# An attention and feed-forward kernel: another cycle of the engines' orders, and other places for the preparations

## The chip, the cores and the metric

The kernel runs on one core of a Trainium2 chip. The time is device microseconds of one execution; of several runs the median is given. The engines of the core are PE (matrix multiply), DVE, ACT and POOL (vector, scalar and general engines) and SP, which issues plain DMA transfers. POOL issues the transfers that add to what lies at their destination.

## The reference

Attention over pooled keys that are also the values, and a feed-forward layer with `h - tanh(h)` between its two products:

```python
kv_pool = kv.reshape(B, H // r, r, W // r, r, C).mean(axis=(2, 4))
k = v = kv_pool.reshape(B, -1, C) @ w_sr
s = scale * (q @ k.transpose(0, 2, 1))
a = np.exp(s - s.max(-1, keepdims=True))
a /= a.sum(-1, keepdims=True) + 1e-09
x = (a @ v).reshape(B * S, D)
h = x @ w_in
return (h - np.tanh(h)) @ w_out
```

B is 4, C is 128, there are 12288 queries and 768 pooled keys for each of the four batches, and the inner width of the feed-forward layer is 2048.

## The kernel before

The 49152 tokens are worked off in 96 groups of 512, 24 to a batch. For each group the kernel does an attention part and a feed-forward part, both written for small arguments: `exps` and `beyond` make the exponential less its straight part, and `square` and `cube` the cubic part of `h - tanh(h)`, while the straight parts are small products with matrices prepared for each batch (`Mh`, `Ah`).

In one group PE does 3 pairs of `scores` (L1073), 3 pairs of `values` (L1122), 8 pairs of `forth` (L1196), 8 pairs of `back` (L1234), two straight products of three (L1112, L1185) and `shares` (L1107), the sum of the attention weights. DVE does 3 `beyond` (L1080), 7 `cube` (L1203) and `apart` (L1133). ACT does 3 `exps`, 7 `square`, `copy`, and copies, among them `result` (L1245), the one that writes a group's output tile. POOL does the eighth piece of the feed-forward part (`moved_pool` L1210, and two `times` L1214, which write z and then rp), and three roundings: `rounded` (L1136), `lower_left` (L1165), `lower_q` (L1116).

For `shares` the three tiles of weights are first added up by transfers. SP copies the first to tile rs (L1093), POOL issues two transfers that add the second and the third to it (`added`, L1096), and from group 8 on one that adds its right half to its left (`folded`, L1099); each of them waits until the one before it has landed, since they write the same tile. `shares` reads the result.

The keys of the batches 1 to 3 are pooled by transfers too: SP loads the first of 16 pieces to tile kvp, and POOL issues 15 that add to it (`gather`, L604), one in each group, 15 groups in a row for each batch. Behind the last of them come the preparations of the batch: sums and products of the keys, the first-order step (`first`, `first_order`), slopes, `scaled` (L947, makes winr), `by_first` (L978, makes Wg) and `by_third` (L998, makes Wr).

The order of all instructions is set when the kernel is built. Each step is entered with a place (a number; 8 to a group), an engine, and a length; `Plan.run` lets the engines work by these lengths, and of the steps that could start it takes the one with the smallest place. The places of a group's steps stand in the table `AT`, those of preparations in `PLACES`; steps entered with `lane=True` keep the order of their places on their engine. An engine works off its steps strictly in the order that comes out of this: a step that waits holds up all that is behind it.

Of the kernel before, what the change touches and what calls it, by code (L numbers as in the profile page):

```python
# [46 lines left out]
class Plan:  # L47

    HOP = 0
# [3 lines left out]
    def __init__(self, tc, places):  # L53
        self.tc = tc
        self.ops, self.tiles, self.rings = [], {}, {}
        self.names = {}
        self.lanes = {}
        self.labels, self.places, self.moved, self.label_of = {}, places, {}, []
# [20 lines left out]
    def op(self, step, engine, us, emit, reads=(), writes=(), late=0.0, port=False, dma=0.0,  # L79
           name=None, lane=False):  # L80
        i = len(self.ops)
        label = self.label(emit, writes)
# [13 lines left out]
    def run(self, between):  # L96
        for t in self.tiles.values():
            i = t["by"][0][0] if t["by"] else None
# [31 lines left out]
        while any(ready.values()):  # L130
# [15 lines left out]
            if dma:  # L146
                free["dma"] = max(free.get("dma", 0.0), now + us) + dma
                late += free["dma"] - (now + us)
# [163 lines left out]
    "store_left left.3": 9.4781431, "copied rs.4": 9.4797277, "store": 9.4807533, "store 2": 9.6811954,  # L312
# [3 lines left out]
    "square W4": 20.156587, "straight acc.2": 20.1579222, "rows norms": 21.113721,  # L316
# [70 lines left out]
def attention_then_ffn(ctx: ExitStack, tc: tile.TileContext, q, kv_first, kv_by_key, kv_by_place,  # L387
# [650 lines left out]
    def attention(g, s0, s1):  # L1038
# [108 lines left out]
        if g >= FOLDED:  # L1147
            plan.op(s0 + AT["folded"], "POOL", 0.87 if g < SET else 0.65, folded, (rs,), (rs,), late=2.0, dma=0.3,
                    lane=True)
# [407 lines left out]
```

## Time and profile before

| what | value |
|---|---|
| median of 3 runs | 1343.48 us (1339.9 to 1345.6) |
| the profiled execution | 1343.29 us, span 1341.6 us |
| PE busy | 1265.1 us (94%) |
| DVE busy | 1209.6 us (90%) |
| ACT busy | 1204.6 us (90%) |
| POOL busy | 1225.6 us (91%) |
| adding transfers (queue q0) | 78.53 MB, 36.6% of the DMA engines' span |
| mean granted clock of PE | 0.997 |

The span is that of the instructions in the trace; the time of the execution holds a little more around it. The busy shares are means over stages of different kinds, so the rows further down cut the span into stages at the starts of `result`. On POOL the recorded spans of neighbours overlap by some tenths of a us, so there the distance from start to start is the length of a step.

### The profile page before, as it was taken

The numbers are of one execution on the slowest core, as the hardware profiler recorded it, in microseconds if no ns is written. First come the engines' busy times: TensorE is split into PE (matmuls) and PEld (weight loads), VectorE is DVE, ScalarE is ACT, GpSimd is POOL, SyncE is SP. The second block draws the span as 40 slices with busy tenths as digits, with TensorE's granted clock in tenths as the row PEclk, the third lists the DMA queues.
The fourth block names the chain that finished last, engine by engine and source line by source line (L and its number), as shares of the span: only waits on it lengthen the run. The fifth ranks groups of instructions, "written<-read, shape, count | busy, mean of one in ns | idle before, by whom it ended". The sixth has DMA issues, their size and how long they took to land.

```text
span 1341.6 us, 17444 instructions
## 1 busy us (share of the span) xinstructions
PE 1265.1 (94%) x5466; PEld 873.0 (65%) x5466; DVE 1209.6 (90%) x1171; ACT 1204.6 (90%) x1413; POOL 1225.6 (91%) x1069
## 2 busy tenths in 40 slices
PE   8999989998989889999989988999999999999997
PEld 6767666766756557666666666766666666666664
DVE  4999998888888888999989988899999999999996
ACT  3899998898889988999989988899999999999995
POOL 3799899999998988999999898899999999999996
PEclk9999999999999999999999999999999999999999
DMA  9286666456666664554666676354544545555541
GB/s 346 61 161 136 145 129 146 99 120 138 140 126 145 122 140 113 122 126 107 145 123 142 129 144 137 81 133 116 124 107 114 126 100 122 122 114 119 122 95 36
DMA packets 95621, 170.01 MB, mean 127 GB/s; under 512 B 11329, under 2 KB 24769, under 8 KB 95521
## 3 DMA queue, kind: packets, MB, share of 16 engines
q0 software_dynamic: 46224, 78.53, 36.6%
q1 hardware_dynamic: 49296, 90.29, 19.1%
q8 instruction: 45, 0.74, 0.2%
q14 instruction: 56, 0.45, 0.1%
HBM read 57.93 MB, written 25.39 MB: 62 GB/s over the span
## 4 chain that ended last, share of the span: by engine, by line
POOL 51%; PE 16%; DMA 15%; issue 11%; DVE 4%; ACT 2%; SPq 0%; POOLq 0%; ACTq 0%; DVEq 0%
POOL rp L1214 13%; DMA rs<-r 12%; POOL rs L1096 9%; POOL z L1214 8%; POOL z L1210 5%; PE big L1196 5%; POOL dl L1165 4%; PE acc L1234 4%; POOL rs L1099 4%; POOL ql L1116 3%; DVE r L1203 2%; POOL dr L1136 2%; PE big L1073 2%; PE x L1122 2%; POOL kvp L604 1%
## 5 line engine op out<-in xcount | busy, mean ns | idle before, releaser
L1203 DVE SCALAR_TENSOR_TENSOR r<-big,u 128x1024 fp32r<-128x1024 f32 x672 | 779.3, 1218 | 35.2 <-ACT u L1200 33.9
L1200 ACT ACTIVATE u<-big 128x1024 f32<-128x1024 f32 x672 | 660.0, 1031 | 45.7 <-PE big L1196 36.0
L1196 PE MATMUL big<-dr,winr 128*128 128x512 f32 x1536 | 531.1, 427 | 2.1 <-DVE r L1080 1.2
L1234 PE MATMUL acc<-r,Wr 128*128 128x512 f32 x1344 | 413.0, 398 | 0.6 <-DVE r L1203 0.6
L1080 DVE SCALAR_TENSOR_TENSOR r<-E,big 128x1024 f16<-128x1024 f32 x288 | 349.3, 1217 | 55.3 <-ACT E L1077 49.3
L1196 PEld LDWEIGHTS big<-dr,winr 128*128 128x128 f32 x1536 | 272.5, 189 | 103.2 <-DVE r L1203 26.0
L1077 ACT ACTIVATE E<-big 128x1024 f32<-128x1024 f32 x288 | 295.6, 1027 | 19.8 <-PE big L1073 13.0
L1234 PEld LDWEIGHTS acc<-r,Wr 128*128 128x128 f32 x1344 | 251.5, 189 | 59.1 <-DVE r L1203 1.5
L1214 POOL TENSOR_TENSOR rp<-z,v 128x1024 fp32r<-128x1024 f32 x96 | 289.5, 3016 | 0.2
L1214 POOL TENSOR_TENSOR z<-z,v 128x1024 f32<-128x1024 f32 x96 | 265.9, 2769 | 0.3
L1096 POOL DMA_DIRECT2D rs<-r x188 | 208.9, 1111 | 31.1 <-DMA rs<-r 13.5
L1073 PE MATMUL big<-qr,kTr 128*128 128x512 f32 x576 | 212.0, 450 | 0.4 <-ACT kTr L720 0.4
L1122 PE MATMUL x<-r,vvr 128*128 128x512 f16 x576 | 174.3, 385 | 0.0
L1116 POOL TENSOR_TENSOR ql<-q,qr 128x512 fp32r<-128x512 f32 x96 | 160.5, 1672 | 0.5 <-ACT qr L1057 0.5
L1165 POOL TENSOR_TENSOR dl<-df,dr 128x512 fp32r<-128x512 f32 x96 | 160.8, 1675 | 0.0
L1210 POOL TENSOR_SCALAR z<-v 128x1024 f32<-128x1024 f32 x96 | 124.5, 1297 | 12.6 <-ACT v L1207 11.9
L1073 PEld LDWEIGHTS big<-qr,kTr 128*128 128x128 f32 x576 | 102.6, 189 | 48.7 <-DVE r L1080 14.5
L1099 POOL DMA_DIRECT2D rs<-rs x88 | 87.9, 998 | 25.4 <-DMA rs<-r 24.4
L1234 PE MATMUL acc<-rp,Wr 128*128 128x512 f32 x192 | 67.2, 431 | 39.7 <-POOL rp L1214 39.3
L1207 ACT COPY v<-big 128x1024 f32<-128x1024 f32 x96 | 97.8, 1019 | 1.8 <-PE big L1196 1.6
L1245 ACT ACTIVATE o<-acc,At 128x512 f32<-128x512 f32 x96 | 65.8, 685 | 29.1 <-PE acc L1234 28.9
L1136 POOL TENSOR_SCALAR dr<-df 128x512 fp32r<-128x512 f32 x96 | 82.4, 858 | 2.7 <-DVE df L1133 2.7
(178 smaller groups left out, 1020.5 us busy)
## 6 DMA issues: line engine op xcount, KB each, us to landing
rs<-r POOLq DMA_DIRECT2D x188, 256.0 KB, 4.1
q<-in_q_dram SPq DMA_DIRECT2D x96, 256.0 KB
out_dram<-o SPq DMA_DIRECT2D x96, 256.0 KB
rs<-r SPq DMA_DIRECT2D x94, 256.0 KB
kvp<-in_kv_by_place_dram POOLq DMA_DIRECT2D x45, 384.0 KB, 5.5
rs<-rs POOLq DMA_DIRECT2D x88, 128.0 KB, 2.7
winr<-in_kv_first_dram SPq DMA_DIRECT2D x8, 384.0 KB
kc<-inverse SPq DMA_DIRECT2D x12, 256.0 KB
```

Of the source, the lines that this page charges most:

```text
L1073: PE.matmul(out=half(plan[s], h), lhsT=plan[kTr][:, n * P : (n + 1) * P], rhs=plan[qr], start=True, stop=True)
L1077: A.activation(out=plan[e], in_=plan[s], func=AF.Exp)
L1080: V.scalar_tensor_tensor(out=plan[r], in0=plan[e], scalar=-1.0, in1=plan[s], op0=ALU.add, op1=ALU.subtract)
L1096: PL.dma_start(out=plan[rs], in_=plan[r2s[k]], accum_op=ALU.add)
L1116: PL.tensor_tensor(out=plan[ql], in0=plan[qs], in1=plan[qr].bitcast(F32), op=ALU.subtract)
L1122: PE.matmul(out=plan[num], lhsT=plan[vvr][:, n], rhs=half(plan[f"r2.{g}.{k}"], h), start=(start and h == 0), stop=(stop and h == 1))
L1165: PL.tensor_tensor(out=plan[dl], in0=plan[df], in1=plan[dr].bitcast(F32), op=ALU.subtract)
L1196: PE.matmul(out=half(plan[hp], h), lhsT=plan[winr][:, f * P : (f + 1) * P], rhs=plan[dr], start=True, stop=True)
L1200: A.activation(out=plan[u], in_=plan[hp], func=AF.Square)
L1203: V.scalar_tensor_tensor(out=plan[r], in0=plan[hp], scalar=1.0, in1=plan[u], op0=ALU.add, op1=ALU.mult)
L1214: PL.tensor_tensor(out=plan[to], in0=plan[x], in1=plan[y], op=ALU.mult)
L1234: PE.matmul(out=plan[acc], lhsT=plan[Wr][:, 2 * n + h], rhs=half(plan[r], h), start=(start and h == 0), stop=(stop and h == 1))
```

## The change

The planner's rules get a queue of their own for transfers that add (`way`): such transfers follow one another there, each beginning no sooner than `AHEAD` behind its issue. The lengths and the times at which results are handed on are set to other values. The table `AT` of a group's places is replaced, and so is a part of `PLACES` (all entries of the preparations of the batches 1 to 3). No step is added or taken away, and no shape is changed.

```diff
-    HOP = 0
+    HOP, AHEAD = 0, 0.85
@@ class Plan, op
+        if way:
+            self.ways.add(i)
@@ class Plan, run
             if dma:
-                free["dma"] = max(free.get("dma", 0.0), now + us) + dma
-                late += free["dma"] - (now + us)
+                way, ahead = ("way", self.AHEAD) if i in self.ways else ("dma", 0.0)
+                free[way] = max(free.get(way, 0.0), now + us + ahead) + dma
+                late += free[way] - (now + us)
@@ PLACES
-    "scaled winr.1 2": 234.4723885, "by_third Wr.1 4": 243.982368, "by_first wg.1.2": 253.4967438,
+    "scaled winr.1 2": 230.002, "by_third Wr.1 2": 230.0025, "by_third Wr.1 4": 230.003,
@@ keys, gather
-            plan.op(at + (0.01 if w else -4), *(("POOL", 0.87 if b < 2 else 0.65) if w else ("SP", 0.5)), gather, (), (kvp,),
-                    late=3.0, dma=1.0, lane=w > 0)
+            if w:
+                plan.op(at + 0.01, "POOL", 0.607, gather, (), (kvp,), late=0.3, dma=3.5, lane=True, way=True)
+            else:
+                plan.op(at - 4, "SP", 0.5, gather, (), (kvp,), late=3.0, dma=1.0)
@@ AT
-        back=[10.761, 7.019, 7.331, 7.954, 6.395, 8.578, 9.358, 5.772], scores=[-20.616, -21.551, -19.32],
+        back=[10.776, 7.328, 7.019, 7.947, 6.399, 8.721, 9.34, 6.09], scores=[-20.605, -21.533, -19.303],
...
-        more=[6.696, 8.691], copied=-18.562, added=[-15.731, -13.315], folded=-9.726, shares=-7.11, left=-6.713,
+        more=[6.68, 8.666], copied=-18.551, added=[-15.755, -12.945], folded=-9.746, shares=-7.434, left=-6.705,
...
-        lower_q=-12.065, lower_left=3.108, gather=-5.737)
+        lower_q=-12.123, lower_left=2.23, gather=-4.52)
@@ attention
-                plan.op(s0 + AT["added"][k - 1], "POOL", 0.87 if g < SET else 0.65, partial(added, k), (r2s[k],), to,
-                        late=2.4, dma=0.6, lane=True)
+                plan.op(s0 + AT["added"][k - 1], "POOL", 0.638, partial(added, k), (r2s[k],), to, late=0.3, dma=1.8,
+                        lane=True, way=True)
...
-            plan.op(s0 + AT["folded"], "POOL", 0.87 if g < SET else 0.65, folded, (rs,), (rs,), late=2.0, dma=0.3,
-                    lane=True)
+            plan.op(s0 + AT["folded"], "POOL", 0.645, folded, (rs,), (rs,), late=0.3, dma=0.9, lane=True, way=True)
```

On POOL, a group with a gather (group 45), from behind the second `times` of the group before to its own, before:

```order
L604 DMA kvp<-in_kv_by_place_dram 128x768
L1096 DMA rs<-r_6938 128x1024
L1165 TENSOR_TENSOR dl<-df,dr 128x512
L1116 TENSOR_TENSOR ql<-q,qr 128x512
L1210 TENSOR_SCALAR z<-v 128x1024
L1136 TENSOR_SCALAR dr<-df 128x512
L1099 DMA rs<-rs 128x512
L1214 TENSOR_TENSOR z<-z,v 128x1024
L1096 DMA rs<-r_7040 128x1024
L1214 TENSOR_TENSOR rp<-z,v 128x1024
```

The same place in the changed kernel, whose line numbers are 4 to 6 higher:

```order
L1170 TENSOR_TENSOR dl<-df,dr 128x512
L1102 DMA rs<-r_6936 128x1024
L608 DMA kvp<-in_kv_by_place_dram 128x768
L1122 TENSOR_TENSOR ql<-q,qr 128x512
L1215 TENSOR_SCALAR z<-v 128x1024
L1142 TENSOR_SCALAR dr<-df 128x512
L1105 DMA rs<-rs 128x512
L1219 TENSOR_TENSOR z<-z,v 128x1024
L1102 DMA rs<-r_7035 128x1024
L1219 TENSOR_TENSOR rp<-z,v 128x1024
```

The step dl (`lower_left`) now stands ahead of the second `added`, and the gather behind it. A plain group reads the same without the gather's row.

On POOL, a group with a preparation (group 36, batch 2), its first six rows before:

```order
L998 TENSOR_TENSOR Wr<-wout_69,hb 128x512
L1096 DMA rs<-r_5671 128x1024
L1165 TENSOR_TENSOR dl<-df,dr 128x512
L1116 TENSOR_TENSOR ql<-q,qr 128x512
L1210 TENSOR_SCALAR z<-v 128x1024
L1136 TENSOR_SCALAR dr<-df 128x512
```

and now:

```order
L1170 TENSOR_TENSOR dl<-df,dr 128x512
L1102 DMA rs<-r_5676 128x1024
L1122 TENSOR_TENSOR ql<-q,qr 128x512
L953 TENSOR_TENSOR winr<-win_67,kc 128x512
L1215 TENSOR_SCALAR z<-v 128x1024
L1142 TENSOR_SCALAR dr<-df 128x512
```

The preparation stood ahead of the second `added` and of `lower_left`; now it stands behind `lower_q`, and it is another one of the batch.

On PE, any plain group from the straight product of the feed-forward part to `shares`, before:

```order
L1185 MATMUL acc<-dl,Ah 128x512
L1196 MATMUL big<-dr,winr 128x512 x2
L1234 MATMUL acc<-r,Wr 128x512 x2
L1196 MATMUL big<-dr,winr 128x512 x2
L1234 MATMUL acc<-r,Wr 128x512 x2
L1196 MATMUL big<-dr,winr 128x512 x2
L1234 MATMUL acc<-r,Wr 128x512 x4
L1196 MATMUL big<-dr,winr 128x512 x2
L1234 MATMUL acc<-r,Wr 128x512 x2
L1196 MATMUL big<-dr,winr 128x512 x2
L1234 MATMUL acc<-r,Wr 128x512 x2
L1107 MATMUL x<-rs,share 128x512
```

and now:

```order
L1190 MATMUL acc<-dl,Ah 128x512
L1201 MATMUL big<-dr,winr 128x512 x4
L1240 MATMUL acc<-r,Wr 128x512 x4
L1201 MATMUL big<-dr,winr 128x512 x2
L1240 MATMUL acc<-r,Wr 128x512 x4
L1201 MATMUL big<-dr,winr 128x512 x2
L1240 MATMUL acc<-r,Wr 128x512 x2
L1201 MATMUL big<-dr,winr 128x512 x2
L1113 MATMUL x<-rs,share 128x512
```

A second pair of `forth` goes ahead of the first `back`, and `shares` stands ahead of the `back` pair that it followed.

## Rows read from the trace of the kernel before

**Rows 1.** Windows by stage, instructions of L1245 alone: stretch, length, ACT busy (groups), clock, DMA.
```profile
96.90:133.60 36.70, 2.04 (x3) 1.00 0.65 141
146.30:227.50 81.20, 4.13 (x6) 1.00 0.67 136
227.50:315.80 88.30, 4.12 (x6) 0.98 0.52 119
315.80:498.80 183.00, 8.96 (x13) 1.00 0.65 134
498.80:650.00 151.20, 7.53 (x11) 1.00 0.52 121
650.00:827.90 177.90, 8.94 (x13) 1.00 0.66 135
827.90:1018.60 190.70, 9.60 (x14) 1.00 0.49 115
...
1108.40:1291.70 183.30, 10.22 (x15) 1.00 0.50 116
```
**Rows 2.** Windows, last stage: PE, PEld, DVE, ACT, POOL busy, clock, DMA.
```profile
1108.40:1291.70 183.30, 183.30 (x767) 124.06 (x766) 181.93 (x166) 180.99 (x211) 174.11 (x136) 1.00 0.50 116
```
**Rows 3.** Timeline of POOL, a gather group: start, us, what, [idle before it].
```profile
427.60 1.49 POOL L604 DMA_DIRECT2D kvp<-in_kv_by_place_dram  x1
429.31 0.85 POOL L1096 DMA_DIRECT2D rs<-r  x1 [0.21 <-issue]
429.87 1.61 POOL L1165 TENSOR_TENSOR dl<-df,dr 128x512 fp32r<-128x512 f32 x1
431.11 1.61 POOL L1116 TENSOR_TENSOR ql<-q,qr 128x512 fp32r<-128x512 f32 x1
432.37 1.36 POOL L1210 TENSOR_SCALAR z<-v 128x1024 f32<-128x1024 f32 x1
433.39 0.92 POOL L1136 TENSOR_SCALAR dr<-df 128x512 fp32r<-128x512 f32 x1
435.28 0.89 POOL L1099 DMA_DIRECT2D rs<-rs  x1 [0.96 <-DMA rs<-r]
435.92 2.67 POOL L1214 TENSOR_TENSOR z<-z,v 128x1024 f32<-128x1024 f32 x1
438.27 1.17 POOL L1096 DMA_DIRECT2D rs<-r  x1
438.88 2.98 POOL L1214 TENSOR_TENSOR rp<-z,v 128x1024 fp32r<-128x1024 f32 x1
441.23 1.46 POOL L604 DMA_DIRECT2D kvp<-in_kv_by_place_dram  x1
```
**Rows 4.** The chain that ended last, the same group: start, us, what.
```profile
429.31 5.68 DMA rs<-r
```
**Rows 5.** L1096 alone, 1150 to 1250 us (plain groups): landings.
```profile
DMA to landing us min/median/max: 3.3/3.6/4.8
```
**Rows 6.** Timeline of POOL, a plain group.
```profile
1164.56 1.21 POOL L1096 DMA_DIRECT2D rs<-r  x1
...
1168.73 0.88 POOL L1096 DMA_DIRECT2D rs<-r  x1 [0.51 <-DMA rs<-r]
...
1173.79 0.88 POOL L1099 DMA_DIRECT2D rs<-rs  x1
```
**Rows 7.** DMA issues, 360 to 500 us: count, size, median us to landing.
```profile
kvp<-in_kv_by_place_dram POOLq DMA_DIRECT2D x10, 384.0 KB, 5.5
rs<-rs POOLq DMA_DIRECT2D x10, 128.0 KB, 2.7
```
**Rows 8.** Groups by line: busy us, mean ns, idle before.
```profile
L947 POOL TENSOR_TENSOR winr<-win,kc 128x512 fp32r<-128x512 f32 x12 | 23.4, 1953 | 0.0
L998 POOL TENSOR_TENSOR Wr<-wout,hb 128x512 fp32r<-128x512 f32 x16 | 22.9, 1438 | 0.8 <-DVE wout L527 0.7
```
**Rows 9.** Timeline of PE, a plain group around the weights' sum.
```profile
1177.24 0.63 PE L1234 MATMUL acc<-r,Wr 128*128 128x512 f32 x2
1177.71 0.39 PE L1107 MATMUL x<-rs,share 128*128 128x512 f16 x1
```

More of the change, by code (lines that the diff above doesn't have):

```diff
@@ L57, in __init__ @@
         self.lanes = {}
+        self.ways = set()
         self.labels, self.places, self.moved, self.label_of = {}, places, {}, []
@@ L79, in op @@
     def op(self, step, engine, us, emit, reads=(), writes=(), late=0.0, port=False, dma=0.0,
-           name=None, lane=False):
+           name=None, lane=False, way=False):
         i = len(self.ops)
+        if way:
+            self.ways.add(i)
         label = self.label(emit, writes)
@@ L278 @@
     "load_words words.o.0": -154.3354073, "load planes.2 2": -149.679321, "load planes.0 2": -145.9573847,
[33 rows of a table removed]
-    "store_left left.3": 9.4781431, "copied rs.4": 9.4797277, "store": 9.4807533, "store 2": 9.6811954,
[3 rows of a table removed]
-    "square W4": 20.156587, "straight acc.2": 20.1579222, "rows norms": 21.113721,
[66 rows of a table removed]
[34 rows of a table added]
+    "straight acc.2": 20.1579222, "rows norms": 21.113721, "square p4.0": 21.4626768,
[69 rows of a table added]
 }
@@ L411, in attention_then_ffn @@
     PAIR, THREE = (0.465, 0.469), (0.7, 0.704)
-    PE_LATE, ACT_LATE, DVE_LATE = (0.196, 0.15), (0.14, 0.1), (0.2, 0.14)
+    PE_LATE, ACT_LATE, DVE_LATE, POOL_LATE = (0.196, 0.186), (0.14, 0.135), (0.2, 0.14), (0.0, 0.38)
     BUFS = {"kc": 2, "kvp": 1, "kTr": 2, "vvr": 2, "Mn": 1, "Mh": 2, "A": 2, "Ah": 2, "Wg": 3, "Wr": 2,
@@ L1028, in attention_then_ffn @@
     AT = dict(
-        forth=[4.008, 1.046, 1.669, 5.46, 0.266, 6.083, 6.707, -0.357],
-        first=[4.466, 1.603, 2.213, 5.871, 0.678, 6.495, 7.119, 0.064],
-        then=[5.134, 2.321, 3.075, 6.548, 1.566, 7.302, 8.057, 0.811],
-        back=[10.761, 7.019, 7.331, 7.954, 6.395, 8.578, 9.358, 5.772], scores=[-20.616, -21.551, -19.32],
-        exps=[-20.144, -21.139, -18.908], beyond=[-19.413, -20.17, -18.232], values=[-3.68, -4.927, -4.304],
-        more=[6.696, 8.691], copied=-18.562, added=[-15.731, -13.315], folded=-9.726, shares=-7.11, left=-6.713,
-        straight=-6.019, apart=-2.656, rounded=-2.118, rounded_q=-24.272, slope=4.992, result=11.47,
-        lower_q=-12.065, lower_left=3.108, gather=-5.737)
+        forth=[4.014, 1.031, 1.693, 5.471, 0.257, 5.78, 6.709, -0.362],
+        first=[4.484, 1.619, 2.225, 5.903, 0.689, 6.509, 7.141, 0.081],
+        then=[5.17, 2.351, 3.101, 6.598, 1.6, 7.349, 8.099, 0.85],
+        back=[10.776, 7.328, 7.019, 7.947, 6.399, 8.721, 9.34, 6.09], scores=[-20.605, -21.533, -19.303],
+        exps=[-20.122, -21.101, -18.871], beyond=[-19.396, -20.148, -18.176], values=[-3.676, -4.914, -4.295],
+        more=[6.68, 8.666], copied=-18.551, added=[-15.755, -12.945], folded=-9.746, shares=-7.434, left=-6.705,
+        straight=-5.998, apart=-2.643, rounded=-2.135, rounded_q=-24.253, slope=5.006, result=11.505,
+        lower_q=-12.123, lower_left=2.23, gather=-4.52)
     def attention(g, s0, s1):
@@ L1153, in attention @@
         plan.op(s1 + AT["left"] + 1, "SP", 0.5, store_left, (t,), (f"left.{g}",), late=2.0, dma=0.02)
-        plan.op(s0 + AT["lower_q"], "POOL", 1.29, lower_q, (qs, qr), (ql,), lane=True)
+        plan.op(s0 + AT["lower_q"], "POOL", 1.25, lower_q, (qs, qr), (ql,), late=POOL_LATE[g >= SET], lane=True)
         terms = [(AT["values"][k], PAIR[g >= SET], partial(values, k), (vvr, r2s[k])) for k in range(AN)]
@@ L1159, in attention @@
             plan.op(s1 + at, "PE", us, partial(emit, start=(n == 0), stop=(n == AN)), of, (num,),
-                    late=PE_LATE[g >= SET], lane=True)
+                    late=PE_LATE[g >= SET] if g < SET or n == AN else 0.0, lane=True)
         plan.op(s1 + AT["apart"], "DVE", 0.6 if g < SET else 0.63, apart, (num, t), (df,), late=DVE_LATE[g >= SET], lane=True)
-        plan.op(s1 + AT["rounded"], "POOL", 0.59, rounded, (df,), (dr,), lane=True)
+        plan.op(s1 + AT["rounded"], "POOL", 0.59, rounded, (df,), (dr,), late=POOL_LATE[g >= SET], lane=True)
         def lower_left():
             PL.tensor_tensor(out=plan[dl], in0=plan[df], in1=plan[dr].bitcast(F32), op=ALU.subtract)
-        plan.op(s1 + AT["lower_left"], "POOL", 1.29, lower_left, (df, dr), (dl,), lane=True)
+        plan.op(s1 + AT["lower_left"], "POOL", 1.25, lower_left, (df, dr), (dl,), late=POOL_LATE[g >= SET], lane=True)
     EARLY = (2.5, 4.4, 4, 6, 8, 18, 24, 8)
@@ L1222, in feed_forward @@
                 plan.op(first, "ACT", 0.905, copy, (hp,), (v,), late=ACT_LATE[g >= SET], lane=True)
-                plan.op(then, "POOL", 1.1, moved_pool, (v,), (z,), lane=True)
+                plan.op(then, "POOL", 1.1 if g < SET else 1.03, moved_pool, (v,), (z,), lane=True)
                 for to, at in zip((z, r), AT["more"]):
-                    plan.op(s0 + at, "POOL", 2.41, partial(times, to, z, v), (z, v), (to,), lane=True)
+                    plan.op(s0 + at, "POOL", 2.37, partial(times, to, z, v), (z, v), (to,),
+                            late=0.5 if to == r and g >= SET else 0.0, lane=True)
             else:
@@ L1241, in feed_forward @@
             plan.op(s0 + at, "PE", us, partial(emit, start=(n == 0), stop=(n == UN)), of, (acc,),
-                    late=PE_LATE[g >= SET], lane=True)
+                    late=PE_LATE[g >= SET] if g < SET or n == UN else 0.0, lane=True)
         def result():
```

203 rows, old and new, of the table PLACES are left out of this document.

## Prediction

> **What bounds the kernel now.** I read first how fast the groups of 512 tokens come out, stage by stage, and then asked in the slow stages which wait ends last. The windows that count the output copies (L1245, one per group) show it [rows 1]. In the last stage 15 groups take 183.3 us, 12.22 each. There PE is busy 183.3 of 183.3 us and DVE 181.9 [rows 2]: both are full, so 12.22 is the floor of a plain group and no order of POOL's work can beat it. Two stages hold nearly only plain groups that also carry one adding load of the keys (`gather`, L604): 6 groups in 81.2 us (13.5 each) and 13 in 177.9 us (13.7 each). Early in the program three groups have such loads too, but no `folded` (it starts with group 8); they take 36.7 us, 12.23 each. So the adding load costs 1.4 us where there is a fold and nothing where there is none: the loss is no bandwidth, it is a loop through the fold.
>
> POOL's order shows that loop [rows 3]. From one L1099 (`folded`) to the next: L1099 to `times` 0.64 us, `times` 2.35, first `added` 0.61, second `times` 2.35 (to the L604 at 441.23), L604 to the second `added` (L1096) 1.71 (427.60 to 429.31), and from that L1096 to the next L1099 5.97. Sum 13.63, the period. In the 5.97 POOL works 4.7 and then waits 0.96 for DMA rs<-r. The chain that ended last goes the same way: 5.68 us of DMA from the second `added` [rows 4]. Where no L604 stands ahead, the same transfer lands after a median of 3.6 us [rows 5], and POOL only waits for the first `added` (0.51 us) [rows 6]. So the load, which lands 5.5 us after its issue [rows 7], holds the `added` behind it for about 2 us, `folded` waits for that, and since POOL works in order everything behind `folded` waits too.
>
> **The change, part by part.** *The gather goes behind the second `added`.* In POOL's order `lower_left` comes up ahead of the second `added`, and the gather falls to just behind it. The loop is then 0.64 + 2.35 + 0.61 + 2.35 + 1.24 (`lower_left`, 429.87 to 431.11) + 3.6 (landing) + 0.3 (5.97 less 5.68, what stands between landing and L1099) = 11.1 us, below 12.22. What is next is POOL's own sum: 0.64 + 2.35 + 0.61 + 2.35 + 1.24 + second `added` 0.56 + gather 1.71 + `lower_q` 1.26 + `moved_pool` 1.02 + `rounded` about 0.6 (0.92 recorded, its record overlaps the next as the others do) = 12.3. The gather's price is the open one: 0.56, as an `added` between two vector steps costs, or 1.71, as the pair of transfers L604, L1096 shows. Two transfers still stand side by side, so I take 1.71. A gather group then takes 12.35 us.
>
> *Plain gather groups.* First stage: 81.2 - 6 x 12.35 = 7.1 us saved. The stage of 13 groups from 650.0: 177.9 - 160.6 = 17.3; I take 16, since the last product of the preparation's slopes moves into it by the new order.
>
> *Gather groups with preparations* (13 groups from 315.8, 183.0 us). POOL also has 4 `by_third`, 1 `by_first`, 3 `scaled` and two small steps there. By record L998 takes 1.44 us and L947 1.95 [rows 8]; less the overlap of 0.64 that the rows of group 3 show (recorded 2.98 and 2.35 apart), 0.8 to 1.3. Together 10 us. In the old order the loop had room for little of that, and with POOL full at 12.3 they now add in whole: 13 x 12.35 + 10 = 170.5; 12.5 saved.
>
> *The three stages without gathers for most groups* (6 groups from 227.5, 11 from 498.8, 14 from 827.9). Each begins with one or two gather groups, which save 1.3 each: 2.6, 3 and 3. The rest of their loss is the chain of the key sums, first-order steps and products on PE, DVE and POOL. Its steps stay the same in number; they are shuffled, with `scaled` and `by_third` now behind `lower_q` and not between the second `times` and the second `added`, so that `lower_left`, for which DVE's `apart` and PE's straight product wait, is not held up by them. I count nothing for it; between -4 and +4 us for each of the three stages is the bound.
>
> *Plain groups.* PE gets a second `forth` ahead of the `back` pairs, and `shares` one `back` pair earlier, 0.47 us (1177.24 to 1177.71) [rows 9]. DVE's and ACT's orders are the same in a plain group. Since DVE and PE are full there, I count no gain and no loss. `shares` needs the fold's landing: L1099 at 1173.79 [rows 6] plus 2.7 [rows 7] is 1176.5, and `shares` starts at 1177.71, so 1.2 us of cover; 0.7 remain.
>
> *Planner's numbers* (`AHEAD`, `way`, the `late` values) issue nothing; they act through the order alone.
>
> **Sum.** 7.1 + 16 + 12.5 + 2.6 + 3 + 3 = 44.2 us. The profiled execution took 1343.3 us (span 1341.6 and 1.7 around it), which is the median of the three runs, 1343.5. 1343.3 - 44.2 = 1299.
>
> **A page against the row.** The second `added` lands 5.68 us after its issue with a gather ahead, 3.6 without, and the gather itself in 5.5 [rows 4, 5, 7]. The Trainium skill ("DMA: Bandwidth & Descriptors", section on the anatomy of one DMA on the SWDGE path) fits a transfer of this path as 2.0 us plus bytes over 436 GB/s: an estimate from it is 2.9 us for 384 KB, so that a gather ahead would hold an `added` for 0.9 us at most. By that rule the old loop would be 0.64 + 2.35 + 0.61 + 2.35 + 1.71 + 3.5 = 11.2 us, it would bind nothing, and the new place would give nothing. This trace does not agree: adding transfers land later than the fit says, and the wait of 0.96 us is there.
>
> **The rivals.**
> (a) *`folded` behind the gather, `shares` late.* From 2.7 us for 128 KB and 3.6 for 256 KB an adding transfer moves 0.9 us per 128 KB after 1.8 of fixed time; the gather, 5.5, moves 3.7. With the second `added` issued at 0, it moves until 3.6, the gather until 7.3, and the fold, issued at about 0.56 + 1.71 + 1.26 + 1.02 + 0.6 = 5.15, lands at 7.3 + 0.9 = 8.2 where 7.85 would be undisturbed: 0.35 late, inside the cover of 0.7. For it: the margin is thin, and landings vary (3.3 to 4.8 in plain groups [rows 5]). If `shares` comes 0.6 us late in each of some 34 gather groups, PE waits 20 us: 1320.
> (b) *The order does not matter to the load.* If the gather holds up whatever is around it, `folded` still waits, at 13.5 a group; only the shuffle of preparations counts: 1343, and 1331 to 1355 at its bounds. Against it: the groups without folds run at 12.23 with the same loads.
> (c) *Slower: the fold's loop in plain groups.* Moving `lower_left` ahead takes 1.24 us from the time between the second `added` and `folded` in every group. The loop is 7.5 us plus the landing. With 3.6 it is 11.1; with a landing of 5.0 it reaches 12.5 and binds in the plain groups too. With x us a group everywhere, 52 plain groups lose x - 12.22 and 34 gather groups win 13.6 - x: the change loses from x = 12.77, a landing of 5.3 us. At 5.5 it gives x = 13.0 and 52 x 0.78 - 34 x 0.6 = +20: 1363. Against it: the largest landing in the plain stage is 4.8.
>
> **How the numbers follow.** Forecast 0.65; (a) 0.20; (b) 0.08; (c) 0.05; 0.02 for anything else. The likeliest case gives 1299; with the stages of preparation at their bounds 1287 to 1311. If all loss of the gather stages goes (7.9 + 24.1 + 19.0 us against 12.22) and the others give 12 in all, the time is 1280, the low end; (a) sets the high end, 1320. A run of this kernel tells about 0.5% from no change. Forecast and (a) are faster by more than that, (b) is the same, (c) slower: 0.87, 0.08, 0.05.
>
> **What would show it.** In the gather stages: 12.3 to 12.4 us a group; L1105, the new line of `folded`, no longer waits for DMA rs<-r; the `added` behind `lower_left` lands in about 3.6 us; POOL is busy nearly without gaps. (a) shows as PE waiting at `shares` for DMA rs<-rs, (b) as 13.5 a group, (c) as POOL waiting at `folded` in the last stage, with more than 12.22 a group there. The forecast is wrong if the last stage's period moves at all, since 0.1 us there is 5 to 9 us over the program, or if the preparations cost more in their new places than they did.

## The result, and the profile after

The changed kernel takes 1321.03 us (median of 4 runs, 1318.29 to 1322.75), the kernel before on the same chip 1343.78 (4 runs): a ratio of 0.9833 [0.9804, 0.9862], 1.7% faster. The forecast was 1299, its range 1280 to 1320: the gain has the forecast's sign and half its size, and the time lies just above the range, at the 1320 that rival (a) gave. The profiled execution took 1322.75 us, the slowest of the four (span 1321.0).

The windows of the changed kernel on `result`, now L1251, between the starts that answer to those of [rows 1] (stretch, length, ACT busy with the number of groups, clock, DMA):

```profile
145.90:226.30 80.40, 4.09 (x6) 0.98 0.67 138
226.30:311.60 85.30, 4.11 (x6) 1.00 0.54 122
311.60:488.30 176.70, 8.90 (x13) 0.99 0.66 139
488.30:640.10 151.80, 7.53 (x11) 1.00 0.52 120
640.10:806.60 166.50, 8.88 (x13) 1.00 0.69 144
806.60:999.30 192.70, 9.60 (x14) 0.99 0.49 113
1087.40:1271.30 183.90, 10.24 (x15) 1.00 0.50 116
```

The gain stands in three stages: the 13 gather groups (177.9 to 166.5 us), the 13 with preparations (183.0 to 176.7), and the second row (88.3 to 85.3). The six gather groups of the first row gain 0.8 only, chiefly since one of them (group 9) grew from 13.73 to 16.11 us, and the two long stages of preparations gain nothing.

POOL's timeline of one gather group, which answers to [rows 3] (start, us, what, idle time before it):

```profile
717.66 0.88 POOL L1102 DMA_DIRECT2D rs<-r  x1 [0.18 <-issue]
718.25 1.22 POOL L608 DMA_DIRECT2D kvp<-in_kv_by_place_dram  x1
718.81 1.97 POOL L1122 TENSOR_TENSOR ql<-q,qr 128x512 fp32r<-128x512 f32 x1
720.32 1.47 POOL L1215 TENSOR_SCALAR z<-v 128x1024 f32<-128x1024 f32 x1
721.34 1.04 POOL L1142 TENSOR_SCALAR dr<-df 128x512 fp32r<-128x512 f32 x1
721.90 1.34 POOL L1105 DMA_DIRECT2D rs<-rs  x1
722.54 3.15 POOL L1219 TENSOR_TENSOR z<-z,v 128x1024 f32<-128x1024 f32 x1
726.17 0.88 POOL L1102 DMA_DIRECT2D rs<-r  x1 [0.47 <-DMA rs<-r]
726.78 2.71 POOL L1219 TENSOR_TENSOR rp<-z,v 128x1024 fp32r<-128x1024 f32 x1
```

`folded` (L1105) waits for nothing here, and only once, for 0.6 us, in the stage's 13 groups (9.0 us in 10 groups before): the loop no longer binds. The waits of that stage (engine, line, what was waited for; us in total, times, the longest) show what came in its place:

```profile
PE x L1113 <- DMA rs<-rs: 6.4, 11, 1.1
PEld L1113 <- DMA rs<-rs: 5.7, 6, 1.5
...
POOL rs L1102 <- DMA rs<-r: 1.7, 4, 0.5
...
POOL rs L1105 <- DMA rs<-r: 0.6, 1, 0.6
```

PE now stands at `shares` (L1113) until the fold has landed, 6.4 us in 11 of the 13 groups. The row of PEld is the weight load of the same step: the same waits, seen from another row, and not to be added. PE's timeline, in the group above:

```profile
724.84 0.62 PE L1201 MATMUL big<-dr,winr 128*128 128x512 f32 x2
726.58 0.39 PE L1113 MATMUL x<-rs,share 128*128 128x512 f16 x1 [1.12 <-DMA rs<-rs]
726.62 0.82 PE L1240 MATMUL acc<-r,Wr 128*128 128x512 f32 x2
```

The landings in that stage, of the fold and of the gather (times from issue to landing):

```profile
L1105 POOL DMA_DIRECT2D rs<-rs x13: 876/1166/1417, 644.7 to 798.4; - x13
DMA to landing us min/median/max: 2.9/3.9/4.6
...
L608 POOL DMA_DIRECT2D kvp<-in_kv_by_place_dram x13: 1216/1529/1871, 640.4 to 794.1; - x13
DMA to landing us min/median/max: 6.4/6.9/7.4
```

The fold, 2.7 us from issue to landing in [rows 7], takes 3.9, and the gather 6.9 instead of 5.5. In the old order both transfers ahead of the fold had landed when it was issued: at 435.28 in [rows 3], against 433.1 (427.60 and 5.5) and 434.99 (429.31 and 5.68); now the gather is issued 0.59 us behind the `added`, and the fold 3.65 us behind the gather, which is still under way. In the last stage, which has no gathers, the busy times of PE, PEld, DVE, ACT and POOL are those of [rows 2]:

```profile
1087.40:1271.30 183.90, 183.46 (x768) 123.54 (x767) 181.98 (x166) 181.23 (x211) 174.63 (x138) 1.00 0.50 116
```

### The profile page after: what moved, and what is told of

Same layout as the page of the kernel before. It is cut to its first block, busy times and chain, and to the rows that moved or that the text cites. A ratio compares the mean times of both kernels' runs of the same rounds, so it can differ in the third digit from the quotient of the medians.

```text
span 1321.0 us, 17453 instructions
## 1 busy us (share of the span) xinstructions
PE 1263.0 (96%) x5466; PEld 877.6 (66%) x5466; DVE 1212.0 (92%) x1171; ACT 1202.6 (91%) x1413; POOL 1228.0 (93%) x1069
## 4 chain that ended last, share of the span: by engine, by line
POOL 47%; PE 29%; issue 9%; DMA 8%; ACT 4%; DVE 3%; POOLq 0%; ACTq 0%; DVEq 0%
POOL rp L1219 11%; POOL rs L1102 9%; PE big L1201 8%; POOL z L1219 8%; PE acc L1240 8%; POOL z L1215 5%; DMA rs<-r 4%; POOL ql L1122 4%; PE big L1079 4%; DMA rs<-rs 3%; PE x L1128 3%; POOL dr L1142 3%; POOL rs L1105 2%; POOL kvp L608 2%; PE x L1118 2%
## 5 line engine op out<-in xcount | busy, mean ns | idle before, releaser
L1201 PE MATMUL big<-dr,winr 128*128 128x512 f32 x1536 | 498.9, 416 | 1.5 <-DVE r L1208 0.5
L1219 POOL TENSOR_TENSOR rp<-z,v 128x1024 fp32r<-128x1024 f32 x96 | 284.2, 2961 | 0.2
L1219 POOL TENSOR_TENSOR z<-z,v 128x1024 f32<-128x1024 f32 x96 | 279.6, 2912 | 0.3
L1102 POOL DMA_DIRECT2D rs<-r x188 | 237.5, 1263 | 17.1 <-DMA rs<-r 13.9
L1079 PE MATMUL big<-qr,kTr 128*128 128x512 f32 x576 | 210.8, 447 | 0.4 <-ACT kTr L726 0.4
L1122 POOL TENSOR_TENSOR ql<-q,qr 128x512 fp32r<-128x512 f32 x96 | 201.9, 2103 | 0.5 <-ACT qr L1063 0.5
L1170 POOL TENSOR_TENSOR dl<-df,dr 128x512 fp32r<-128x512 f32 x96 | 174.7, 1820 | 0.0
L1215 POOL TENSOR_SCALAR z<-v 128x1024 f32<-128x1024 f32 x96 | 127.6, 1329 | 30.9 <-ACT v L1212 30.8
L1079 PEld LDWEIGHTS big<-qr,kTr 128*128 128x128 f32 x576 | 102.0, 189 | 50.5 <-DVE r L1086 19.3
L1105 POOL DMA_DIRECT2D rs<-rs x88 | 101.3, 1151 | 2.4 <-DMA rs<-r 1.7
L1142 POOL TENSOR_SCALAR dr<-df 128x512 fp32r<-128x512 f32 x96 | 85.9, 895 | 0.0
L1128 PEld LDWEIGHTS <-vvr 128*128 128x128 f16 x576 | 33.6, 98 | 78.0 <-issue 77.5
```

The lines of the kernel that those rows point to most:

```text
L1079: PE.matmul(out=half(plan[s], h), lhsT=plan[kTr][:, n * P : (n + 1) * P], rhs=plan[qr], start=True, stop=True)
L1102: PL.dma_start(out=plan[rs], in_=plan[r2s[k]], accum_op=ALU.add)
L1122: PL.tensor_tensor(out=plan[ql], in0=plan[qs], in1=plan[qr].bitcast(F32), op=ALU.subtract)
L1128: PE.matmul(out=plan[num], lhsT=plan[vvr][:, n], rhs=half(plan[f"r2.{g}.{k}"], h), start=(start and h == 0), stop=(stop and h == 1))
L1201: PE.matmul(out=half(plan[hp], h), lhsT=plan[winr][:, f * P : (f + 1) * P], rhs=plan[dr], start=True, stop=True)
L1215: PL.tensor_scalar(out=plan[z], in0=plan[v], scalar1=1.0, scalar2=1.0, op0=ALU.add, op1=ALU.mult)
```

## The experiments

Nine kernels were run, each against the kernel before on the same chip. Its medians there were 1341.4 to 1342.3 us, 1.5 to 2.4 below those beside the changed kernel, so differences of medians between runs are good to some 2 us, and the ratios are the better comparison. The stages are named by the groups that they hold, counted from 0: 6 to 11 (gathers), 12 to 23 and 24 to 30 (gathers from 18, and preparations), 31 to 41 (preparations), 42 to 54 (gathers), 55 to 68 (preparations), 76 to 90 (plain).

### 1. `shares` back in its old place

```diff
-        ... folded=-9.746, shares=-7.434, left=-6.705,
+        ... folded=-9.746, shares=-7.11, left=-6.705,
```

> The changed kernel with the place of shares put back (-7.11), so that PE does one more pair of back ahead of it (0.47 us). Theory A (the fold's transfer moves behind the gather's, lands 1.2 us later than in plain groups, and PE stands still at shares until then): the wait at shares falls by about 0.4 us in each of some 34 gather groups, about 14 us in all, and the long waits get shorter: 1305 to 1310 us. Theory B (POOL's own sum of 12.3 us or more sets the gather groups, and the wait at shares is only where the slack of PE shows): 1318 to 1323 us.

1311.32 us, ratio 0.9768 [0.9735, 0.9801]: 10 us faster than the changed kernel by the medians and 9 by the ratios, just above theory A's 1305 to 1310 and well below theory B's 1318. The windows on `result`, of the groups 6 to 11, 12 to 17, 18 to 30, 31 to 41, 42 to 54 and 55 to 68:

```profile
145.40:221.90 76.50, 4.10 (x6) 1.00 0.69 145
221.90:307.70 85.80, 4.10 (x6) 1.00 0.54 122
307.70:480.50 172.80, 8.91 (x13) 1.00 0.68 142
480.50:634.00 153.50, 7.52 (x11) 0.99 0.52 119
634.00:798.10 164.10, 8.88 (x13) 1.00 0.70 146
798.10:988.40 190.30, 9.59 (x14) 1.00 0.50 115
```

and the waits of the gather stage:

```profile
PEld acc L1240 <- POOL rp L1219: 7.2, 12, 1.0
...
PEld L1113 <- DMA rs<-rs: 2.5, 6, 1.1
...
PE x L1113 <- DMA rs<-rs: 0.7, 1, 0.7
```

The fold still lands in 3.7 us at the median there, but one pair of `back` later PE stands at `shares` in one group only (0.7 us in place of 6.4 in the stage). What PE waits for next is POOL's rp. POOL is busy 162.96 of the 164.10 us, and seven of the 13 groups take 12.47 to 12.51 us: that is POOL's own sum. The three stages with gathers give back 10.2 us (80.4 to 76.5, 176.7 to 172.8, 166.5 to 164.1), about the whole difference (9.7 between the medians).

### 2 and 3. `shares` later still

```diff
-        ... shares=-7.434, left=-6.705, straight=-5.998,
+        ... shares=-6.85, left=-6.3, straight=-5.5,
```

> The changed kernel with shares two pairs later on PE (place -6.85), the copy of its result one square later on ACT (left at -6.3), and the straight product of the attention behind the next scores (-5.5), since both use one bank. Theory A: 0.94 us of cover more, which takes nearly all of the wait at shares out of the gather groups: about 1298 us, 12.3 to 12.5 us a gather group. Theory B: 1318 to 1323 us. If the later copy makes the straight product wait for the bank instead, plain groups take more than 12.22 us and the time is above 1321.

```diff
-        ... shares=-7.434, left=-6.705, straight=-5.998,
+        ... shares=-6.85, left=-6.6, straight=-5.998,
```

> The changed kernel with shares two pairs later on PE (place -6.85), and nothing else moved but left from -6.705 to -6.6. With shares one pair later the gather groups took 12.5 us and POOL's sum set them, so theory A leaves little for one pair more: it only takes the last waits at shares, 1307 to 1312 us. If the copy behind shares, and with it the straight product that needs its bank, comes late, plain groups take more than 12.22 us and the time is 1315 us or more.

1340.89 us, ratio 0.9992 [0.9978, 1.0006], and 1326.66, 0.9889 [0.9872, 0.9907]. The plain groups, full before, get longer: 12.73 and 12.61 in place of 12.22. Nearly all gather groups of 42 to 54 take as long as these (12.8 and 12.68 on average), no less than in the first run. In the plain stage of the second run PE stands at `scores` (L1079) for DVE's `cube`, which it does not in the changed kernel:

```profile
PE big L1079 <- DVE r L1208: 5.7, 15, 0.4
```

That is most of the 7.1 us by which this stage is longer. In the third run PE shows no gap (189.20 of 189.20 us busy), but its weight loads wait 5.0 us for `cube` at `scores` and 2.9 us at the straight product (L1118) for the copy behind `shares`; the changed kernel has neither. So the times lie where the last branch of each expectation put them, but the wait that it named, for the bank, shows in the third run alone and in part. More cover at `shares` is paid for in every group, and the old place is the best of the four kernels tried. Why `cube` comes late there was not told apart.

### 4. Half of each gather

```diff
-    PL.dma_start(out=plan[kvp], in_=kv_by_place[b - 1, w], accum_op=ALU.add)
+    PL.dma_start(out=plan[kvp][:, 0:KH], in_=kv_by_place[b - 1, w, :, 0:KH], accum_op=ALU.add)
```

The sums of the other half of the keys are left out, from the second piece on.

> The changed kernel with each adding load of the keys cut to the first half of its columns (the sums of the other half are left out): as many issues on POOL, half the bytes. Theory A: the load moves for about 1.9 us and not 3.7, the fold lands in about 2.7 us as in plain groups, no wait at shares: 12.3 us a gather group, about 1296 us. Theory B: the issues stay, and with them POOL's sum: 1318 to 1322 us.

1307.53 us, 0.9741 [0.971, 0.9773], with `shares` in the changed kernel's early place. The landings of the fold and of the gather in the groups 42 to 54:

```profile
DMA to landing us min/median/max: 2.7/3.0/4.2
...
DMA to landing us min/median/max: 5.3/5.7/7.5
```

With 192 KB ahead of it the fold is 0.3 us late and not 1.2, and the gather lands 1.2 us sooner (6.9 to 5.7). By the Trainium skill ("DMA: Bandwidth & Descriptors", section on the anatomy of one DMA on the SWDGE path: 2.0 us plus bytes over 436 GB/s) an estimate for 192 KB less is 0.45 us; the runs do not agree, and the measurement decides. The gather groups take 12.58, and POOL is busy 162.78 of the stage's 163.40 us. That they take no less, with half of the bytes, says that POOL's sum bounds them now and not the queue. The time lies between the two numbers expected: 13.5 us below the changed kernel (12 by the ratios), which is over half of the 22 us that were missing. So the fold's delay is most of the loss, and not all.

### 5. The gather ahead of the second `added` again

```diff
-        lower_q=-12.123, lower_left=2.23, gather=-4.52)
+        lower_q=-12.123, lower_left=2.23, gather=-5.0)
```

> The changed kernel with the gather put ahead of the second added again (place -5.0), with lower_left still ahead of both. The loop of the prediction (folded, times, added, times, lower_left, gather, added and its landing behind the gather, folded) is 0.64 + 2.35 + 0.61 + 2.35 + 1.24 + 1.71 + 5.97 = 14.9 us: gather groups go from about 12.9 to 14.9 us, 36 of them, so about 1390 us, and POOL waits at folded for the second added. If the loop was not what bound the gather groups, 1316 to 1326 us.

1399.12 us, 1.0427 [1.0393, 1.0461]; 15.04 a group in the groups 42 to 54. The waits there:

```profile
POOL rs L1105 <- DMA rs<-r: 28.7, 12, 3.4
PEld L1113 <- DMA rs<-rs: 27.3, 11, 3.5
...
PE x L1113 <- DMA rs<-rs: 22.6, 11, 3.0
```

With `lower_left` moved up, the gather's new place is what keeps the loop through the fold from binding. The arithmetic of the loop, taken from rows of before, gave 14.9; the program took 9 us more than the 1390 expected. The gather's new place without that of `lower_left` was not run.

### 6 to 8. One part of the change alone

The sixth is the changed kernel with the places of preparations of before (`PLACES`), the seventh the changed kernel with the cycle of before (`AT`), the eighth the kernel before with the three values that reorder POOL:

```diff
-        added=[-15.731, -13.315] ... lower_left=3.108, gather=-5.737
+        added=[-15.731, -12.945] ... lower_left=2.23, gather=-4.52
```

> The changed kernel with the places of the preparations as they were before (all of PLACES), and the new cycle. Theory A (the new cycle alone makes the gain, the places of the preparations neither give nor take): 1317 to 1325 us, with the stages around the batches' ends as long as in the changed kernel. Theory C (the new places cost something there, which eats part of the gain, as the 192.7 us against 190.7 in the 14 groups of batch 3's preparation hint): 1308 to 1315 us. Theory D (the new places are needed for the new cycle): above 1328 us.

> The changed kernel with the table of a group's places as it was before, and the new places of the preparations and the new lengths. Theory A: POOL's order in a gather group is the old one, so the loop through folded is back, 13.5 us a gather group: 1338 to 1346 us. Theory D (the places of the preparations carry the gain): 1320 to 1328 us.

> The kernel before with three numbers of the table changed: the place of the second added (-12.945), of lower_left (2.23) and of the gather (-4.52). POOL's order in a gather group is then that of the changed kernel, PE's is the old one, with shares behind its back pair. Theory A: the loop is gone and shares has its cover, as with the changed kernel and shares put back: 1308 to 1316 us. If the rest of the new table or the new places matter: 1320 us or more.

| kernel | us | ratio | groups 42 to 54, each |
|---|---|---|---|
| new cycle, old places | 1346.24 | 1.0037 [1.002, 1.0053] | 13.10 |
| old cycle, new places | 1344.55 | 1.0021 [1.001, 1.0032] | 13.58 |
| before, POOL's three values | 1341.5 | 0.9994 [0.998, 1.0009] | 12.94 |

With the old cycle `folded` waits again, in the same stage:

```profile
POOL rs L1105 <- DMA rs<-r: 11.0, 13, 1.3
```

With the old places the loop is gone, but single groups at the end of a batch of gathers become very long: 23.38 us in group 31 and 25.08 in group 55, where the changed kernel has 15.33 and 18.2. The chain of the sixth kernel around group 31, in order of time:

```profile
488.71 6.20 DMA kvp<-in_kv_by_place_dram
495.05 2.90 PE big L654 x4
```

PE's first product of the batch's keys (L654) stands in its order ahead of steps of the groups, and now finds the last gather, which is issued later in its group, still under way. PE waits there, and all its steps behind it. The eighth kernel has the same in group 31 (22.82 us), and in group 21 (28.8 us) PE stands at the slopes, L985 in its lines, for the Wg that POOL makes:

```profile
PE x L985 <- POOL Wg L978: 9.2, 1, 9.2
```

So each part alone gains nothing over the program, since what it wins in the gather groups is lost in single long groups, or, with the old cycle, the loop is back. Together they gain 22 us. Of the expectations theory D came true for the sixth kernel, theory A for the seventh, and the last branch (1320 us or more) for the eighth.

### 9. Every `by_third` twice, on the first run's kernel

```diff
-                PL.tensor_tensor(out=plan[Wr][:, fs], ...)
+                for _ in range(2 if b else 1):
+                    PL.tensor_tensor(out=plan[Wr][:, fs], ...)
```

> The changed kernel with shares in its place of before (the run with 1311 us), and every by_third of the batches 1 to 3 issued twice in a row: the second writes the same numbers again, 12 more instructions on POOL, each about 1.0 us from start to start; the order is otherwise the same. Theory A: the stages of preparations gained nothing because POOL's own sum fills them, so each repeat costs its full 1.0 us: the stage from group 31 to 42 goes from 153.5 to about 157.5 us, that from 55 to 69 from 190.3 to about 194, the groups 17 to 23 lose about 4, and the time is 1321 to 1324 us. Theory B: the chain of the key sums, products and slopes on PE and DVE bounds these stages, and POOL has room there: the stages stay within 1 us and the time is 1311 to 1314 us.

1327.59 us, 0.9892 [0.9871, 0.9913]. The stage of the groups 31 to 41 goes from 153.5 to 156.6 us, that of 55 to 68 from 190.3 to 194.6, and the groups 12 to 23 from 169.2 to 173.3: 11.5 in all. The groups 36 to 38, each with one repeat, go from 13.73, 13.54 and 13.54 to 14.86, 14.64 and 14.63. POOL's timeline in one of them:

```profile
576.60 1.46 POOL L984 TENSOR_TENSOR Wg<-winT,hb 128x512 f32<-128x512 f32 x1
577.60 2.58 POOL L1005 TENSOR_TENSOR Wr<-wout,hb 128x512 fp32r<-128x512 f32 x2
580.15 1.06 POOL L1216 TENSOR_SCALAR z<-v 128x1024 f32<-128x1024 f32 x1
```

Nothing is between the steps. The same three groups of the changed kernel have POOL busy (the last before the clock) for their whole time, while PE (the first) is not:

```profile
559.50:600.50 41.00, 38.89 (x171) 27.15 (x169) 36.98 (x35) 37.60 (x46) 41.00 (x35) 1.00 0.51 120
```

Theory A holds: POOL is what bounds these groups. Its expected time, 1321 to 1324, was too low; the medians differ by 16.3 us, the profiled spans (1310.0 and 1323.9) by 13.9, and the twelve repeats by 11.5 in the three stretches; the rest was not attributed.

## Why the prediction was wrong

**The loop, and the floor: right.** The wait of `folded` went as it was said to, and it comes back with the gather's old place alone (fifth kernel) and with the whole cycle of before (seventh). The plain stage moved by 0.6 us in 184. One reading was off without effect: of the 5.97 us from the second `added` to `folded` POOL works 5.0 by its records [rows 3], not 4.7.

**The step that failed** is the weighing of the first rival: the fold "0.35 late, inside the cover of 0.7". Its mechanism stood in the text, with a chance of 0.20, and its size was off. The fold is 1.2 us late at the median of that stage (3.9 for 2.7), up to 1.9, and PE stands 6.4 us at `shares` in 11 of 13 groups. In the timeline above the `added` is issued at 717.66 and the gather at 718.25; the gather took 7.0 us, so it is in 7.6 us after the `added` (7.3 in the prediction). The fold is issued 4.24 after the `added` (4.84 in the group before) and not 5.15, since the gather and `lower_q` took 2.07 us there from start to start (2.67 in the group before), not 1.71 + 1.26. It took 4.6 us and landed just ahead of PE's start at 726.58: some 8.9 after the `added`, not 8.2, and 1.3 behind the gather, not 0.9. PE was ready at 725.46 (726.58 less 1.12), 7.8 after the `added`; the prediction's cover, taken from a plain group, puts that at 8.55 (5.15 + 2.7 + 0.7). So the fold landed 0.7 us later than worked out, and `shares` was due 0.75 sooner.

**Where the cover went.** "Since DVE and PE are full there, I count no gain and no loss" for `shares` one pair earlier holds in plain groups alone. In gather groups these 0.47 us of lost cover cost some 10 us over the program (first run). With that move undone, the forecast would have been 12 us off. That the time meets the 1320 of rival (a) is in part luck: there all 20 us are waits at `shares`, while here the move of `shares` cost some 10 us, the savings missing in the stages of preparations 8, and POOL's sum 4 to 5.

**The three stages of preparations: 8.6 us forecast, 0.4 there.** The prediction gave the one or two gather groups at their start 1.3 us each, as if nothing else stood in them. The stages gained 3.0, -0.6 and -2.0: the first came as forecast, the third is 5.0 us below its forecast and outside the bound of 4. The ninth run shows why there was nothing to win in the middle groups: POOL's sum with two more steps fills 13.5 us, before and after. The trace of before had it (POOL busy 53.47 of 54.0 us from 570.3 to 624.3), and the prediction took the loss for that of a chain through three engines, which holds for none of the groups that were tested. What bounds the first groups of these stages (31 to 33 take 45.5 us, 46.1 before) was not tested.

**POOL's sum.** 12.35 was forecast, 12.47 to 12.51 is what most undisturbed gather groups take in the first run; over the 32 groups of the forecast that is 4 to 5 us.

| stage (groups) | forecast saving | changed kernel | first run |
|---|---|---|---|
| 6 to 11 | 7.1 | 0.8 | 4.7 |
| 12 to 17 | 2.6 | 3.0 | 2.5 |
| 18 to 30 | 12.5 | 6.3 | 10.2 |
| 31 to 41 | 3 | -0.6 | -2.3 |
| 42 to 54 | 16 | 11.4 | 13.8 |
| 55 to 68 | 3 | -2.0 | 0.4 |
| 76 to 90 | 0 | -0.6 | -0.7 |

The savings are the lengths in [rows 1] less those of the windows above (184.0 for the last stage of the first run). The remaining 2.3 us of the profiled executions' difference (1343.3 to 1322.75, 20.6) lie between these stages.

**The shuffled preparations, "I count nothing for it".** With the new places the three stages moved by the 3.0, -0.6 and -2.0 us above. But the gain of the new cycle hangs on these places, and the prediction did not say so. With the gather later in its group, the old places cost 25.2 us (1346.24 less 1321.03; 27 by the ratios), 15 of them in the two long groups; the rest was not attributed. The prediction looked at POOL's steps there and not at PE's, which wait for the last gather.

**What stays open.** In three very long groups of the profiled execution PE stood over 2 us at `shares`: 9, 27 and 55 took 16.11, 15.84 and 18.2 us (the first run: 13.25, 13.07 and 16.35; before, group 55 took 17.29). Their gathers landed after 8.8, 8.8 and 8.5 us and their folds after 5.9, 5.6 and 5.6. The transfers around group 9 (183 to 201 us: packets, MB, share) hold one packet of queue q8, which the profile calls that of instructions:

```profile
q8 instruction: 1, 0.02, 0.3%
```

In these three gather groups, and in no other of the changed kernel, such a packet began while the gather and the fold were both under way. But the first run has five such packets, and none of those five gathers took longer than 7.3 us. So this is a coincidence in one trace, and the cause isn't settled.

## What to carry to other kernels

A transfer that is moved to where it blocks nothing still holds up the next one of its queue: work out the whole queue over one period, with issue times from the trace, and compare with the cover of the last reader in the groups that it is about, which must not be cut in the same change. When a stage's groups are long, look first whether one engine is busy for all of that time; where POOL was, another order of its steps won nothing here. A table of places fits the times of one cycle: test a new cycle and its new places together, since either alone may show nothing.

## What the runs showed of the hardware beyond that

In group 9 the gather landed after 8.8 us and the fold after 5.9. PE stood for 2.38 us, and what followed it ran at a lower clock. Its windows (PE, PEld, DVE, ACT, POOL busy, then granted clock):

```profile
192.00:195.00 3.00, 0.62 (x4) 0.18 (x3) 3.00 (x3) 1.67 (x2) 0.97 (x2) 1.00 0.27 49
195.00:198.00 3.00, 3.00 (x8) 2.41 (x9) 0.14 (x1) 1.54 (x2) 3.00 (x3) 0.55 0.64 117
```

and the chain of the same stretch:

```profile
189.04 5.89 DMA rs<-rs
...
195.36 0.81 PE acc L1240 x2
196.17 0.85 PE big L1201 x2
197.02 0.85 PE acc L1240 x2
...
199.47 0.48 PE big L1079 x2
```

A pair of products takes 0.85 us there, and 0.48 at 199.47: the granted clock was at the lower level, 1.2 GHz, from 0.3 us behind the end of the stand for some 3.4 us. So this wait of 2.4 us cost more than its own length, some 1.5 us more for the four pairs from 195.36 on. The other two stands of over 2 us, 2.1 us each in the groups 27 and 55, were followed by such a stretch too. The stand of 1.12 us ahead of 726.58 was not: the next pairs start 0.48 us apart, at 727.27 and 727.75. Nor was one of 2.30 us in the sixth kernel, ahead of 195.13: the granted clock is 1.00 from 195.2 to 198.2.
